# Three real products per complex product in the half-precision transforms of a state-space and SwiGLU kernel

## The chip, the cores and the metric

The kernel runs on one core of a Trainium2 chip. The metric is the device time of one execution in microseconds (us). The kernel before was run three times: 1212.44, 1216.55 and 1213.18 us, median 1213.18. A profiled execution of it has a span of 1210.1 us from its first to its last instruction.

The engines are named as the profile names them: PE is the matrix engine (PEld its weight loads), DVE the vector engine, ACT the scalar engine, POOL the GpSimd engine, SP the engine that issues most DMAs. Each engine works through its own queue in order.

## The reference

The input x has 2048 rows of 512 channels. Two layers with the same weights follow each other; each is a state-space convolution and a SwiGLU network, both with a layer norm before and a residual after:

```python
K = jnp.einsum("dn,dnl,dn->dl", Cc, P, dB).real          # P = exp(dt * A * l), complex, 128 states
Yf = rfft2(pad(u)) * rfft2(pad(K))                        # convolution over 2048 rows
y = irfft2(Yf)[..., :L] + u * Dskip
x = x + ssm(layernorm(x));   x = x + (silu(n @ w_gate) * (n @ w_up)) @ w_down   # n = layernorm(x), twice
```

The hidden width of the SwiGLU part is 1376. Everything is float32.

## The kernel before

The rows are cut into four blocks b of 512 (`T`), the channels into two halves h of 256 (`HD`). The convolution is done block by block with transforms of length 1024: the frequencies fall into four classes q of 128, and a class is one 128x128 complex matrix. For each layer, block, half and class the following is done, called a step here.

- `forward` (L229) mixes the four 128-row pieces of the normalized block on DVE into `bt` and then into the two real halves `z` (128x2x256) of a complex tile. `z` is split into a float16 part made by ACT (L250) and a float16 remainder made by DVE (L251). Twelve matmuls (four real products, each with three terms of the high and low parts, L260) give the spectrum `pf`, which ACT copies out as `u` (L262). `u` is also stored to `udr` by a DMA on POOL's queue (L637), for later blocks.
- `ssm` (L640) takes the spectra of this block and of the earlier ones and multiplies them by the kernel's spectra: `yk` and `t` hold all four real products of a complex one (128x1024, L683), L686 adds them over the blocks, and L687 and L688 make the complex result `y`, which lies in `yc`, a tile of its own. `y` is split into float16 parts `yl` by ACT (L691) and DVE (L692); twelve matmuls (L702) give the inverse transform `pi`. `combine` (L652) takes `pi` from the matrix engine's memory with one copy by ACT or two operations by DVE. After four classes, 14 operations on tiles of 256 columns (L717 to L731) add the result to x.
- `ffn` (L790) is the SwiGLU part in two pieces of 256 rows: every product is three float16 matmuls (`pgu`, L807 to L809, and `py`, L821 to L823). `pgu` goes through ACT (`sg`, L812), DVE (L813), ACT (`hh`, L814) and DVE (`hl`, L815). DVE adds `py` to x (L826).

The eight pairs of layer and block run in the order of `SEQ` (L42). For each of them the state-space part of the next pair is written ahead of the SwiGLU part of this one, so that both overlap. The first part of the program (the kernel's spectra, until about 355 us) has an order written out by hand; the rest is put in order by the framework's scheduler, which fills each engine's queue once, when the program is built. `tc.high_priority(offset=BOOST)` moves the matmuls of the transforms and the SwiGLU part's elementwise operations ahead. The forward half-precision transform is used from the third pair on (six pairs, 48 steps), the inverse one from the second (seven pairs, 56 steps). The first two pairs' spectra come from the hand-ordered part.

`BUFS` (L83) says how many buffers a name has: `y1` (the tile `yk`) and `z` have one, `t1` three; the small tiles of the matrix engine's memory (`psml`, L92) have four.

Line numbers in the profile are those of the kernel that was profiled; the changed kernel's are about ten higher.

Of the kernel before, what the change touches and what calls it, by code (L numbers as in the profile page):

```python
# [22 lines left out]
P = 128  # L23
# [4 lines left out]
HD = D // 2  # L28
# [8 lines left out]
NA = 21  # L37
TB = 256
BOOST = 1 << 20
HALF = 2  # L40
INV = 1
SEQ = ((0, 0), (0, 1), (0, 2), (1, 0), (0, 3), (1, 1), (1, 2), (1, 3))  # L42

# [1 line left out]
def dft_constants():  # L45


    j = np.arange(P)[:, None]
    r = np.arange(P)[None, :]
    ef = np.zeros((P, 4, 3, P), np.float64)  # L50
    ei = np.zeros((P, 4, 3, P), np.float64)
    ek = np.zeros((P, 4, 3, 2, P), np.float64)
    for q in range(4):
        f = q + 8 * r + 0.5
        e = np.exp(-2j * np.pi * ((j * f) / 1024.0))
        ef[:, q, 0], ef[:, q, 1], ef[:, q, 2] = e.real, e.imag, -e.real
# [12 lines left out]
    return [a.astype(np.float32) for a in (ef, ei, ek, am)] + halves  # L69
# [3 lines left out]
def kernel(ctx, tc, x, a_re, a_im, b_re, b_im, c_re, c_im, log_dt, d_skip,  # L73
# [148 lines left out]
            nc.sync.dma_start(xt, xdr[b].rearrange("c p d -> p c d"))  # L222

    def norm_x(n):
        rs, nb = row_stats(n, 4, 1.0, "stats", lambda r: tl([P, D], "junk", "t1", BF16))
        for c in range(4):
            A.activation(n[:, c], n[:, c], AF.Identity, scale=rs[:, c:c + 1], bias=nb[:, c:c + 1])

    def forward(n, h, eh):  # L229


        hs = slice(h * HD, (h + 1) * HD)
        x0, x1, x2, x3 = (n[:, c, hs] for c in range(4))
# [4 lines left out]
        A.activation(hx, x2, AF.Copy, scale=HH)  # L238
        stt(p_, x3, TT, x1, OP.add)
        stt(r_, x3, -TT, x1, OP.add)  # L240
        stt(q_, x1, TT, x3, OP.subtract)
        stt(s_, x1, TT, x3, OP.add)
        for i, q in enumerate(QORD):
            z = z2[:, 0 if eh else i % 2]
# [3 lines left out]
            if eh:  # L248
                hl = z2[:, 1].bitcast(F16).rearrange("p i (l d) -> p l i d", l=2)
                A.activation(hl[:, 0], z, AF.Copy, scale=256.0)  # L250
                stt(hl[:, 1], z, 256.0, hl[:, 0], OP.subtract)  # L251
            pf = psml([P, 2, HD], "pf")
            with tc.high_priority(offset=BOOST):
                for o in range(2):
                    if eh:
                        terms = [(eh[:, q, o + i, le], hl[:, lz, i]) for i in range(2) for le, lz in ((0, 0), (0, 1), (1, 0))]
                    else:
                        terms = [(ef[:, q, o + i], z[:, i]) for i in range(2)]
                    for k, (e, m) in enumerate(terms):
                        PE.matmul(pf[:, o], lhsT=e, rhs=m, start=k == 0, stop=k == len(terms) - 1)  # L260
                u = tl([P, 2, HD], "u", "u")
                A.activation(u, pf, AF.Copy, scale=2.0 ** -16 if eh else 1.0)  # L262
            yield q, u

    def norm_early(xt, n, factors):
        rs, nb = factors
# [344 lines left out]
    def inputs():  # L611

        for layer, b in SEQ:
# [14 lines left out]
            n = tl([P, 4, D], "n", "n")  # L628
            load_x(n, layer, b)
            norm_x(n)  # L630
            if (layer, b) == SEQ[HALF]:
                eh.append(tl([P, 4, 3, 2, P], "eh", "ef", F16))
                nc.sync.dma_start(eh[0], c_eh)
            for h in range(2):
                for q, u in forward(n, h, eh[0] if eh else None):
# [4 lines left out]
    def ssm(layer, b):  # L640
# [7 lines left out]
        for h in range(2):  # L648
# [3 lines left out]
            def combine(q, pi, bb=bb):  # L652
                if q < 2:
                    bb[q] = tl([P, 2, HD], "bb", "bb")
                    A.activation(bb[q], pi, AF.Copy, scale=sy[:, 1:2] if half else 1.0)
                    return
                s = bb[3 - q]
                bb[q] = tl([P, 2, HD], "dd", "dd")
                if half:
                    stt(bb[q], pi, sy[:, 2:3], s, OP.add)  # L660
                    stt(s, pi, sy[:, 1:2], s, OP.add)
                else:
                    V.tensor_tensor(bb[q], s, pi, OP.subtract)
                    V.tensor_tensor(s, s, pi, OP.add)

            late = []
            for _ in range(4):
# [5 lines left out]
                y = tl([P, 2, HD], "yf", "w") if first else yc  # L673
                for k in range(b + 1):
                    if k == 0:
                        w, uu = w0r[:, h, q], u
# [7 lines left out]
                                    w.unsqueeze(2).to_broadcast([P, 2, 2, HD]), OP.mult)  # L684
                    if k:
                        V.tensor_tensor(yk, yk, t, OP.add)  # L686
                V.tensor_tensor(y[:, 0], yk[:, 0, 0], yk[:, 1, 1], OP.subtract)  # L687
                V.tensor_tensor(y[:, 1], yk[:, 0, 1], yk[:, 1, 0], OP.add)  # L688
                if half:
                    yl = yl2[:, QORD.index(q) % 2]  # L690
                    A.activation(yl[:, 0], y, AF.Copy, scale=sy[:, 0:1])  # L691
                    stt(yl[:, 1], y, sy[:, 0:1], yl[:, 0], OP.subtract)  # L692
                pi = psml([P, 2, HD], "pi")
                with tc.high_priority(offset=0 if first else BOOST):
                    for o in range(2):
                        if half:
                            terms = [(eih[:, q, 0 if i == o else 1 + o, le], yl[:, ly, i])
                                     for i in range(2) for le, ly in ((0, 0), (0, 1), (1, 0))]
                        else:
                            terms = [(ei[:, q, 0 if i == o else 1 + o], y[:, i]) for i in range(2)]  # L700
                        for k, (e, m) in enumerate(terms):
                            PE.matmul(pi[:, o], lhsT=e, rhs=m, start=k == 0, stop=k == len(terms) - 1)  # L702
# [143 lines left out]
    with tc.manual_schedule(engines={mybir.EngineType.Activation, mybir.EngineType.DVE, mybir.EngineType.PE}):  # L846
# [205 lines left out]
    yl2 = tl([P, 2, 2, 2, HD], "yl2", "hf", F16)  # L1052
    xs[2] = tl([P, 4, D], "xf", "xf")
    for i, lb in enumerate(SEQ):
        if i + 1 < len(SEQ):
# [40 lines left out]
```

## Time and profile before

| what | before |
|---|---|
| median of three runs | 1213.18 us (1212.44 to 1216.55) |
| span of the profiled execution | 1210.1 us |
| PE busy | 1104.0 us (91%), 10220 matmuls |
| DVE busy | 1048.5 us (87%), 1677 instructions |
| ACT busy | 646.3 us (53%), 1392 instructions |
| POOL busy | 187.8 us (16%), 209 instructions |

The profile does not list a time of the profiled execution beside its span; the span is 3.1 us below the median of the three runs. "Busy" counts the time in which at least one instruction of an engine was under way. A row that groups instructions reads: line, engine, operation, output<-inputs, shape, count | busy us in total, mean ns of one | idle time of the engine just before them, and what ended it. A matmul's own duration (274 ns for 256 columns) is longer than the distance between two of them, since they are pipelined; a run of them in the chain of waits gives the distance. Times of POOL instructions are rough.

### The profile page before, as it was taken

Reading aid. Unit: us, or ns where it says so; the run is one execution under the profiler, and the core shown is the slowest. Engines: PE = TensorE matmul, PEld = TensorE weight load, DVE = VectorE, ACT = ScalarE, POOL = GpSimd, SP = SyncE. Lnnn points to the kernel's source line nnn. Section 1 sums busy time; section 2 is a strip of 40 time slices with the busy share of each in tenths; the row PEclk is TensorE's granted clock in tenths of the full one; section 3 lists DMA queues with packets and bytes.
Section 4 is the critical chain, followed back from the end, with each engine's and each line's share of the span. In section 5 each row is a group of like instructions: output and inputs, shape, how many; then the busy total and the mean of one; then the engine's idle time right before and its main releaser. Section 6 shows DMA issues by size and latency. Waiting matters only on the chain.

```text
span 1210.1 us, 25368 instructions
## 1 busy us (share of the span) xinstructions
PE 1104.0 (91%) x10220; PEld 858.5 (71%) x10220; DVE 1048.5 (87%) x1677; ACT 646.3 (53%) x1392; POOL 187.8 (16%) x209
## 2 busy tenths in 40 slices
PE   3877988888978998989999999999999999999998
PEld 2755766666976776868686777778686776867875
DVE  8999999999869999999998999999992799983221
ACT  7999999973265545526753524664431553324111
POOL 1116343453220010101100000121000010000000
PEclk9999998889999999999999999999999999999999
DMA  6223233236389427433245353424433144311000
GB/s 226 96 88 92 72 89 86 73 107 184 116 285 264 127 67 199 133 118 88 62 157 140 105 179 133 125 79 146 140 118 129 33 119 132 117 58 44 14 23 18
DMA packets 134857, 138.66 MB, mean 115 GB/s; under 512 B 75921, under 2 KB 85137, under 8 KB 134738
## 3 DMA queue, kind: packets, MB, share of 16 engines
q1 hardware_dynamic: 132178, 128.64, 35.4%
q0 software_dynamic: 2560, 8.39, 2.0%
q8 instruction: 80, 1.31, 0.5%
q14 instruction: 39, 0.32, 0.1%
HBM read 98.71 MB, written 28.31 MB: 105 GB/s over the span
## 4 chain that ended last, share of the span: by engine, by line
DVE 32%; PE 27%; issue 5%; DMA 4%; ACT 2%; POOL 2%; SPq 1%; DVEq 0%; ACTq 0%; POOLq 0%
DVE t L683 5%; PE pgu L807 5%; PE pgu L808 5%; PE pgu L809 5%; DVE yk L686 4%; DVE z L216 3%; DVE yk L683 3%; PE py L821 3%; PE py L822 3%; PE py L823 3%; PE pi L702 2%; DVE sg L813 2%; DVE hl L815 1%; DVE yl L216 1%; DVE bt L216 1%
## 5 line engine op out<-in xcount | busy, mean ns | idle before, releaser
L807 PE MATMUL pgu<-mix,wsl 128*128 128x256 f16 x1280 | 350.5, 274 | 7.9 <-DVE sg L813 4.4
L809 PE MATMUL pgu<-mix,wsl 128*128 128x256 f16 x1280 | 350.5, 274 | 1.2 <-DVE wsl L579 1.2
L808 PE MATMUL pgu<-mix,wsl 128*128 128x256 f16 x1280 | 350.4, 274 | 0.0
L808 PEld LDWEIGHTS <-wsl 128*128 128x128 f16 x1280 | 125.8, 98 | 24.6 <-issue 8.6
L821 PE MATMUL py<-wsl,hh 128*128 128x512 f16 (+1 forms) x352 | 134.6, 382 | 9.3 <-DVE xg L826 5.3
L809 PEld LDWEIGHTS <-wsl 128*128 128x128 f16 x1280 | 125.8, 98 | 16.5 <-DVE wsl L579 1.5
L807 PEld LDWEIGHTS <-wsl 128*128 128x128 f16 x1280 | 125.8, 98 | 15.8
L823 PE MATMUL py<-wsl,hl 128*128 128x512 f16 (+1 forms) x352 | 134.4, 382 | 2.4 <-DVE hl L815 2.4
L812 ACT ACTIVATE sg<-pgu,sc 128x512 f32<-128x512 f32 x80 | 54.5, 682 | 128.8 <-PE pgu L809 110.9
L822 PE MATMUL py<-wsl,hh 128*128 128x512 f16 x320 | 122.1, 382 | 0.0
L683 DVE TENSOR_TENSOR t<-uu,w 128x1024 f32<-128x1024 f32 x96 | 116.8, 1217 | 5.5 <-DMA uu<-udr 5.3
L686 DVE TENSOR_TENSOR yk<-yk,t 128x1024 f32<-128x1024 f32 x96 | 116.7, 1215 | 0.1
L493 PE MATMUL pw<-kt,ek 128*128 128x256 f32 (+2 forms) x420 | 105.4, 392 | 0.0
L813 DVE SCALAR_TENSOR_TENSOR sg<-pgu,sc,sg 128x512 f32<-128x512 f32 x80 | 59.6, 744 | 52.3 <-ACT sg L812 52.0
L702 PE MATMUL pi<-yl,mix 128*128 128x256 f16 x672 | 91.4, 273 | 5.5 <-ACT yl L691 3.5
L493 PEld LDWEIGHTS pw<-kt,ek 128*128 128x128 f32 x420 | 83.9, 208 | 11.9
L814 ACT ACTIVATE hh<-sg 128x512 f16<-128x512 f32 x80 | 50.0, 626 | 67.6 <-DVE sg L813 67.6
L211 POOL TENSOR_TENSOR rs<-mv,mhalf 128x2 f32<-128x2 f32 (+1 forms) x21 | 38.7, 1845 | 275.7 <-ACT mv L210 275.6
L260 PE MATMUL pf<-z,eh 128*128 128x256 f16 x576 | 74.4, 272 | 1.6 <-ACT z L250 1.6
L702 PEld LDWEIGHTS <-mix 128*128 128x128 f16 x672 | 65.3, 98 | 14.3 <-issue 3.9
L691 ACT ACTIVATE yl<-mix,sy 128x512 f16<-128x512 f32 x56 | 40.2, 717 | 61.4 <-DVE mix L688 61.2
L504 POOL COPY w0r<-s 128x128 f32<-128x128 f32 x29 | 48.1, 1659 | 141.7 <-ACT s L502 122.2
(221 smaller groups left out, 2292.0 us busy)
## 6 DMA issues: line engine op xcount, KB each, us to landing
w<-wdr SPq DMA_DIRECT2D x96, 256.0 KB, 2.8
uu<-udr SPq DMA_DIRECT2D x96, 256.0 KB, 3.0
udr<-u POOLq DMA_DIRECT2D x32, 256.0 KB, 2.8
wdr<-wo SPq DMA_DIRECT2D x96, 64.0 KB, 2.0
udr<-u SPq DMA_DIRECT2D x16, 256.0 KB, 2.5
n<-ndr SPq DMA_DIRECT2D x16, 256.0 KB, 3.0
n<-xdr SPq DMA_DIRECT2D x4, 1024.0 KB, 6.0
xg<-in_A_u_dram SPq DMA_DIRECT2D x3, 1024.0 KB, 7.4
```

Of the source, the lines that this page charges most:

```text
L260: PE.matmul(pf[:, o], lhsT=e, rhs=m, start=k == 0, stop=k == len(terms) - 1)
L493: PE.matmul(pw[:, i], lhsT=e, rhs=kt[:, :, c + 4 * k0:4 * k1:4, :].rearrange("p g k d -> p k g d"), start=c == 0, stop=c == 3)
L683: V.tensor_tensor(t, uu.unsqueeze(1).to_broadcast([P, 2, 2, HD]), w.unsqueeze(2).to_broadcast([P, 2, 2, HD]), OP.mult)
L686: V.tensor_tensor(yk, yk, t, OP.add)
L702: PE.matmul(pi[:, o], lhsT=e, rhs=m, start=k == 0, stop=k == len(terms) - 1)
L807: PE.matmul(o, lhsT=wgu(wi, k, 0)[:, fs], rhs=nh[:, k], start=k == 0, stop=False)
L808: PE.matmul(o, lhsT=wgu(wi, k, 0)[:, fs], rhs=nlo[:, k], start=False, stop=False)
L809: PE.matmul(o, lhsT=wgu(wi, k, 1)[:, fs], rhs=nh[:, k], start=False, stop=k == 3)
L813: V.scalar_tensor_tensor(sg, pgu[:, 1], sc6[:, 4:5], sg, OP.mult, OP.mult)
L821: PE.matmul(py[:, r], lhsT=hh[:n, f, rc], rhs=wd(f, 0)[:n], start=f == 0, stop=False)
L822: PE.matmul(py[:, r], lhsT=hh[:n, f, rc], rhs=wd(f, 1)[:n], start=False, stop=False)
L823: PE.matmul(py[:, r], lhsT=hl[:n, f, rc], rhs=wd(f, 0)[:n], start=False, stop=f == FT - 1)
```

## The change

Each complex product of the two half-precision transforms is done with three real products in place of four. For a complex number with the parts z0 and z1 and a matrix with the parts fr and fi, the forward transform becomes

    first part  = (fr - fi) z0 + fi (z0 + z1)
    second part = (-fr - fi) z1 + fi (z0 + z1)

and the inverse one has the same form. The tables `eh` and `eih` hold these three matrices. A new function `three` issues nine matmuls (three real products of three terms): two products go into `pb`, the shared one into `pa`; ACT copies both out, and POOL adds `a` to both halves. The sum z0+z1 and its float16 split are made by POOL in the forward transform (`zsum`, in the place of `yc`); in the inverse one POOL makes the sum, and ACT and DVE split three tiles of 256 columns at once. `y` now lies in `yk` itself. The factor 256, which was applied when `z` was split, is now in the layer norm of `norm_x`. `yl` has one buffer of three parts in place of two buffers of two.

```diff
-    for e in (ef * 256.0, ei * 8192.0):
+    fr, fi, ir, ii = ef[:, :, 0], ef[:, :, 1], ei[:, :, 0], ei[:, :, 1]
+    for e in (np.stack([fi, fr - fi, -fr - fi], 2) * 256.0, np.stack([ir, ii - ir, -ir - ii], 2) * 8192.0):
...
-        rs, nb = row_stats(n, 4, 1.0, "stats", lambda r: tl([P, D], "junk", "t1", BF16))
+        rs, nb = row_stats(n, 4, 256.0, "stats", lambda r: tl([P, D], "junk", "t1", BF16))
...
+        zs, hs2 = zsum[:, 0], zsum[:, 1].bitcast(F16).rearrange("p (l d) -> p l d", l=2)
...
-                A.activation(hl[:, 0], z, AF.Copy, scale=256.0)
-                stt(hl[:, 1], z, 256.0, hl[:, 0], OP.subtract)
-            pf = psml([P, 2, HD], "pf")
+            A.activation(hl[:, 0], z, AF.Copy)
+            V.tensor_tensor(hl[:, 1], z, hl[:, 0], OP.subtract)
+            G.tensor_tensor(zs, z[:, 0], z[:, 1], OP.add)
+            G.tensor_copy(hs2[:, 0], zs)
+            G.tensor_tensor(hs2[:, 1], zs, hs2[:, 0], OP.subtract)
             with tc.high_priority(offset=BOOST):
-                ... (12 matmuls into pf)
                 u = tl([P, 2, HD], "u", "u")
-                A.activation(u, pf, AF.Copy, scale=2.0 ** -16 if eh else 1.0)
+                three(eh[:, q], (hl[:, :, 0], hl[:, :, 1], hs2), u, 2.0 ** -16)
             yield q, u
+
+    def three(e, parts, o, scale):
+        pb = psml([P, 2, HD], "pb")
+        pa = psml([P, 2, HD], "pa")
+        for d, w, m in ((pb[:, 0], 1, parts[0]), (pb[:, 1], 2, parts[1]), (pa[:, 0], 0, parts[2])):
+            for k, (le, lz) in enumerate(((0, 0), (0, 1), (1, 0))):
+                PE.matmul(d, lhsT=e[:, w, le], rhs=m[:, lz], start=k == 0, stop=k == 2)
+        a = tl([P, HD], "a", "t1")
+        A.activation(o, pb, AF.Copy, scale=scale)
+        A.activation(a, pa[:, 0], AF.Copy, scale=scale)
+        G.tensor_tensor(o, o, a.unsqueeze(1).to_broadcast([P, 2, HD]), OP.add)
...
+                if half:
+                    y = yk.rearrange("p a b d -> p (a b) d")[:, :3]
+                    V.tensor_tensor(y[:, 0], yk[:, 0, 0], yk[:, 1, 1], OP.subtract)
+                    V.tensor_tensor(y[:, 1], yk[:, 0, 1], yk[:, 1, 0], OP.add)
+                    G.tensor_tensor(y[:, 2], y[:, 0], y[:, 1], OP.add)
+                    yl = tl([P, 2, 3, HD], "yl", "hf", F16)
+                    A.activation(yl[:, 0], y, AF.Copy, scale=sy[:, 0:1])
+                    stt(yl[:, 1], y, sy[:, 0:1], yl[:, 0], OP.subtract)
+                    bb[q] = tl([P, 2, HD], "bb", "bb") if q < 2 else tl([P, 2, HD], "dd", "dd")
+                    with tc.high_priority(offset=BOOST):
+                        three(eih[:, q], [yl[:, :, i] for i in (1, 0, 2)], bb[q], sy[:, 1:2])
+                    if q > 1:
+                        s = bb[3 - q]
+                        V.tensor_tensor(s, s, bb[q], OP.add)
+                        stt(bb[q], bb[q], -2.0, s, OP.add)
+                    yield
+                    continue
...
-        yc = mix[:, 3 * D:4 * D].rearrange("p (i d) -> p i d", i=2)
+        zsum = mix[:, 3 * D:4 * D].rearrange("p (i d) -> p i d", i=2)
```

The instructions stand in these orders, at three places.

DVE, the 28th inverse step (pair (0, 3), third earlier block), from the end of `y` on; `yl` is the float16 remainder, `yk<-u,w0r` the first product of the next step, `sg` and `hl` the SwiGLU part's. Before:

```order
L687 TENSOR_TENSOR mix<-yk 128x256
L688 TENSOR_TENSOR mix<-yk 128x256
L683 TENSOR_TENSOR t<-uu,w 128x1024
L683 TENSOR_TENSOR yk<-u,w0r 128x1024
L216 SCALAR_TENSOR_TENSOR yl_3763<-mix,sy,yl_3763 128x512
L813 SCALAR_TENSOR_TENSOR sg<-pgu,sc_92,sg 128x512
L686 TENSOR_TENSOR yk<-yk,t 128x1024
L815 TENSOR_TENSOR hl<-sg,hh 128x512
```

and in the change:

```order
L691 TENSOR_TENSOR yk<-yk 128x256
L692 TENSOR_TENSOR yk<-yk 128x256
L685 TENSOR_TENSOR t<-uu,w 128x1024
L824 SCALAR_TENSOR_TENSOR sg<-pgu,sc_92,sg 128x512
L216 SCALAR_TENSOR_TENSOR yl<-yk,sy,yl 128x768
L826 TENSOR_TENSOR hl<-sg,hh 128x512
L685 TENSOR_TENSOR yk<-u,w0r 128x1024
L688 TENSOR_TENSOR yk<-yk,t 128x1024
```

The next step's first product stood ahead of the remainder `yl`; now it stands behind it, and `yl` is half as wide again.

POOL, where the spectra of the second layer's first pair (`udr_115`) are stored: before, a stretch with the stores of `u`, the exponent of a layer norm (`rs<-mv,mhalf`) and the clearing of `sgr`:

```order
L211 TENSOR_TENSOR rs<-mv,mhalf 128x2
L637 DMA udr_114<-u 128x512 x4
L211 TENSOR_TENSOR rs<-mv,mhalf 128x4
L781 MEMSET sgr 128x4x32
L637 DMA udr_114<-u 128x512
L637 DMA udr_115<-u 128x512 x4
```

and in the change (`mix<-z` is the sum z0+z1, `mix<-mix` its two float16 parts, `yk<-yk` the sum of `y`, `u<-u,a` and `bb<-bb,a` the additions of the shared product):

```order
L693 TENSOR_TENSOR yk<-yk 128x256
L254 TENSOR_TENSOR mix<-mix 128x256
L270 TENSOR_TENSOR u<-u,a 128x512
L252 TENSOR_TENSOR mix<-z_3762 128x256
L644 DMA udr_115<-u 128x512
L253 CAST mix<-mix 128x256
L254 TENSOR_TENSOR mix<-mix 128x256
L693 TENSOR_TENSOR yk<-yk 128x256
L252 TENSOR_TENSOR mix<-z_3762 128x256
L211 TENSOR_TENSOR rs<-mv,mhalf 128x2
L270 TENSOR_TENSOR bb<-bb,a 128x512
L270 TENSOR_TENSOR u<-u,a 128x512
```

Each forward step has brought four operations to POOL's queue and each inverse step two; the layer norm's exponent and the stores stand between them.

PE, from the last matmul of the last inverse transform on: before,

```order
L702 MATMUL pi<-yl_3763,mix 128x256
L809 LDWEIGHTS wsl_3322
L809 MATMUL pgu<-mix,wsl_3322 128x256
L807 LDWEIGHTS wsl_3322
L807 MATMUL pgu<-mix,wsl_3322 128x256
```

and in the change:

```order
L266 MATMUL pa<-yl,mix 128x256
L832 LDWEIGHTS hh
L832 MATMUL py<-wsl_3324,hh 128x512
L833 LDWEIGHTS hh
L833 MATMUL py<-wsl_3324,hh 128x512
```

Behind the last inverse matmul stood 988 matmuls, in the middle of the second last pair's SwiGLU part; now there are 741, and they begin with the last output products of that part.

More of the change, by code (lines that the diff above doesn't have):

```diff
@@ L39 @@
 BOOST = 1 << 20
-HALF = 2
 INV = 1
@@ L242, in forward @@
         stt(s_, x1, TT, x3, OP.add)
+        zs, hs2 = zsum[:, 0], zsum[:, 1].bitcast(F16).rearrange("p (l d) -> p l d", l=2)
         for i, q in enumerate(QORD):
-            z = z2[:, 0 if eh else i % 2]
+            z = z2[:, 0]
             u_, v_ = ((p_, a_) if q in (0, 3) else (q_, b_))
@@ L630, in inputs @@
             norm_x(n)
-            if (layer, b) == SEQ[HALF]:
+            if not eh:
                 eh.append(tl([P, 4, 3, 2, P], "eh", "ef", F16))
@@ L634, in inputs @@
             for h in range(2):
-                for q, u in forward(n, h, eh[0] if eh else None):
+                for q, u in forward(n, h, eh[0]):
                     if b < NB - 1:
@@ L654, in combine @@
                     bb[q] = tl([P, 2, HD], "bb", "bb")
-                    A.activation(bb[q], pi, AF.Copy, scale=sy[:, 1:2] if half else 1.0)
+                    A.activation(bb[q], pi, AF.Copy)
                     return
@@ L658, in combine @@
                 bb[q] = tl([P, 2, HD], "dd", "dd")
[L659 to L664, printed above, removed]
+                V.tensor_tensor(bb[q], s, pi, OP.subtract)
+                V.tensor_tensor(s, s, pi, OP.add)
             late = []
@@ L672, in ssm @@
                 yk = tl([P, 2, 2, HD], "yk", "y1")
-                y = tl([P, 2, HD], "yf", "w") if first else yc
                 for k in range(b + 1):
@@ L687, in ssm @@
+                y = tl([P, 2, HD], "yf", "w")
                 V.tensor_tensor(y[:, 0], yk[:, 0, 0], yk[:, 1, 1], OP.subtract)
                 V.tensor_tensor(y[:, 1], yk[:, 0, 1], yk[:, 1, 0], OP.add)
[L689 to L692, printed above, removed]
                 pi = psml([P, 2, HD], "pi")
[L694 to L702, printed above, removed]
+                for o in range(2):
+                    terms = [(ei[:, q, 0 if i == o else 1 + o], y[:, i]) for i in range(2)]
+                    for k, (e, m) in enumerate(terms):
+                        PE.matmul(pi[:, o], lhsT=e, rhs=m, start=k == 0, stop=k == len(terms) - 1)
```

11 lines of the change are left out of this document (1 added, 10 removed).

## The prediction

> **What bounds the kernel now.** I read first the page's busy times, then a table by stage, cut where the stretches with another bound begin.
>
> ```profile
> PE 1104.0 (91%) x10220; PEld 858.5 (71%) x10220; DVE 1048.5 (87%) x1677; ACT 646.3 (53%) x1392; POOL 187.8 (16%) x209
> ```
>
> ```profile
> core 0: us, PE busy (x) PEld busy (x) DVE busy (x) ACT busy (x) POOL busy (x), PEclk, DMA share, GB/s
> 0.00:395.00 395.00, 317.88 (x3666) 254.31 (x3667) 373.15 (x561) 297.90 (x718) 129.16 (x143) 0.94 0.45 137
> 395.00:907.00 512.00, 491.72 (x4144) 384.10 (x4142) 499.77 (x844) 253.45 (x495) 50.95 (x56) 0.99 0.41 125
> 907.00:952.00 45.00, 44.41 (x373) 33.53 (x370) 15.46 (x29) 17.27 (x37) 1.34 (x1) 1.00 0.29 95
> 952.00:1082.00 130.00, 126.88 (x1055) 95.08 (x1053) 123.11 (x184) 44.80 (x83) 4.59 (x5) 1.00 0.35 104
> 1082.00:1210.10 128.10, 123.12 (x992) 91.43 (x989) 36.98 (x62) 32.90 (x60) 1.80 (x4) 0.99 0.09 25
> ```
>
> The average of 91% and 87% hides who leads. From 395 to 907 us DVE is busy 499.8 of 512 us, PE nearly as much. From 907 to 952 DVE stands for 29.5 us, and the timeline of DVE says for what:
>
> ```profile
> 925.46 0.75 DVE L826 SCALAR_TENSOR_TENSOR xg<-py,sc,xg 128x512 f32<-128x512 f32 x1 [5.41 <-PE py L823]
> 940.94 0.75 DVE L813 SCALAR_TENSOR_TENSOR sg<-pgu,sc,sg 128x512 f32<-128x512 f32 x1 [7.31 <-ACT sg L812]
> ```
>
> It waits for PE to finish a SwiGLU part that is late. Then DVE is full again until the last inverse transform at 1082 us, and 128 us of SwiGLU work on PE remain. So DVE sets the pace of the transforms, and PE has a backlog, paid once at 907 (29.5 us) and once at the end. POOL is nearly empty after 395 us.
>
> **PE: what goes.** The distance between the transforms' matmuls stands in the chain of waits:
>
> ```profile
> 539.16 1.31 PE pf L260 x12
> 1081.17 1.20 PE pi L702 x11
> ```
>
> That is 109 ns each. Of the groups by line
>
> ```profile
> L702 PE MATMUL pi<-yl,mix 128*128 128x256 f16 x672 | 91.4, 273 | 5.5 <-ACT yl L691 3.5 <-DVE yl L216 2.0
> L260 PE MATMUL pf<-z,eh 128*128 128x256 f16 x576 | 74.4, 272 | 1.6 <-ACT z L250 1.6
> ```
>
> a quarter goes: 168 + 144 = 312 matmuls, 34 us of PE. Where DVE leads, they are worth nothing.
>
> **DVE: its own work.** The rows:
>
> ```profile
> L686 DVE TENSOR_TENSOR yk<-yk,t 128x1024 f32<-128x1024 f32 x96 | 116.7, 1215 | 0.1
> L216 DVE SCALAR_TENSOR_TENSOR yl<-mix,sy,yl 128x512 f16<-128x512 f32 x56 | 41.6, 743 | 2.2 <-ACT yl L691 2.1
> L216 DVE SCALAR_TENSOR_TENSOR z<-z 128x512 f16<-128x512 f32 x48 | 32.8, 683 | 2.1 <-ACT z L250 2.1
> L815 DVE TENSOR_TENSOR hl<-sg,hh 128x512 f16<-128x512 f32 x80 | 54.8, 684 | 14.0 <-ACT hh L814 13.9
> L216 DVE SCALAR_TENSOR_TENSOR dd<-pi,sy,bb 128x512 f32<-128x512 f32 x28 | 20.8, 743 | 3.5 <-PE pi L702 3.4
> ```
>
> 512 further columns cost 1215 - 684 = 531 ns, so `yl` with 256 more costs 0.27 us more, 56 times: +15 us. The two operations that combined `pi` (743 ns each) become two in the style of the rows of 684 and 683 ns: 28 x 0.12 = -3 us. The remainder of `z` changes from a row of 683 to one of 684 ns: nothing. Own work: **+12 us**.
>
> **POOL, and what it does to DVE.** The change brings 48 x 4 + 56 x 2 = 304 operations to POOL. What one costs alone is seen at 335 us, where DVE has nothing to do:
>
> ```profile
> 335.14 0.32 POOL L513 TENSOR_TENSOR wo<-s,w0r 128x64 f32<-128x64 f32 x1
> 335.42 0.46 POOL L514 TENSOR_TENSOR wo<-s 128x128 f32<-128x128 f32 x1
> ```
>
> 2.2 ns an element and 0.18 us beside: 0.74 us for 256 columns with two inputs, 1.3 us for 512. The one-input cast lies between 0.3 us (the shortest copy of 128 columns, 0.29 below) and 0.74; I take 0.43. A forward step is 3.2 us, an inverse step 2.0 us, 268 us in all, and POOL has some 700 us for it. Would that be all, it would be free. It isn't, by the groups and the timeline of the stretch in which POOL and DVE worked side by side:
>
> ```profile
> L445 DVE TENSOR_TENSOR g<-g,tmp 128x64 f32<-128x64 f32 x8 | 3.4, 425 | 0.0
> L445 DVE TENSOR_TENSOR g<-g,tmp 128x128 f32<-128x128 f32 x8 | 2.3, 284 | 0.0
> L510 POOL TENSOR_TENSOR wo<-s 128x192 f32<-128x192 f32 x58 | 61.8, 1085 | 0.0
> L504 POOL COPY w0r<-s 128x128 f32<-128x128 f32 x29 | 48.1, 1659 | 141.7 <-ACT s L502 122.2 <-DMA st<-in_B_w_up_dram 16.4 <-DMA wdr<-wo 3.0
> ```
>
> ```profile
> 160.74 0.27 DVE L430 TENSOR_TENSOR g<-g,tmp 128x64 f32<-128x64 f32 x1
> 164.05 0.68 DVE L445 TENSOR_TENSOR g<-g,tmp 128x64 f32<-128x64 f32 x1
> 164.65 0.69 DVE L446 TENSOR_TENSOR g<-g,tmp 128x64 f32<-128x64 f32 x1
> ```
>
> ```profile
> 162.76 0.29 POOL L504 COPY w0r<-s 128x128 f32<-128x128 f32 x1 [2.90 <-ACT s L502]
> 163.01 2.19 POOL L510 TENSOR_TENSOR wo<-s 128x192 f32<-128x192 f32 x2
> ```
>
> A DVE operation on half the elements takes longer, on average, than the full one. In the timeline each of the two POOL operations adds 0.41 us to the DVE operation beside it (0.68 for 0.27), and takes 1.1 us itself where 0.18 + 192 x 2.2 ns = 0.60 would do. So here an addition on POOL and a DVE operation with two inputs from the same memory exclude each other, for 0.41 / 192 = 2.1 ns an element, and who comes second waits. The copies of 128 columns took 1659 ns on average, and DVE operations beside copies are not longer, so I give the cast 0.2 us, between nothing and 0.55.
>
> DVE's time that this may take: a forward step 0.55 (sum) + 0.2 + 0.55 (remainder) + 1.09 (the addition of 512 columns) = 2.4 us, 48 times 115 us; an inverse step 0.55 + 1.09 = 1.64 us, 56 times 92 us. Together 207 us: the upper end. Nothing is the lower end, if all falls into DVE's pauses or beside operations with one input from there:
>
> ```profile
> L813 DVE SCALAR_TENSOR_TENSOR sg<-pgu,sc,sg 128x512 f32<-128x512 f32 x80 | 59.6, 744 | 52.3 <-ACT sg L812 52.0
> L826 DVE SCALAR_TENSOR_TENSOR xg<-py,sc,xg 128x512 f32<-128x512 f32 x24 | 17.9, 746 | 37.8 <-PE py L823 37.8
> ```
>
> These are about 75 us in the stretch, of which I let half hide POOL work, 37 us; the pauses from 395 to 907 and from 952 to 1082 are 12 + 7 us, half of them 10; half of the new pause below, 35. Seen on DVE: 207 - 82 = **+125 us**.
>
> **The new wait.** `y` now lies in `yk`, so the next step's first product can't start before `yl` is done, and `yl` waits for POOL's sum and a split by ACT of 768 columns. In the order DVE starts a `t` product of 1.14 us right behind `y`, which shuts POOL out for that long. Then 0.74 us on POOL, and ACT:
>
> ```profile
> L691 ACT ACTIVATE yl<-mix,sy 128x512 f16<-128x512 f32 x56 | 40.2, 717 | 61.4 <-DVE mix L688 61.2
> L379 ACT ACTIVATE re<-im 128x1024 f32<-128x1024 f32 x16 | 17.6, 1102 | 6.4 <-DVE im L372 6.3
> L262 ACT ACTIVATE u<-pf 128x512 f32<-128x512 f32 x48 | 28.3, 589 | 58.8 <-PE pf L260 58.7
> L238 ACT ACTIVATE bt<-n 128x256 f32<-128x256 f32 x12 | 4.9, 407 | 9.0 <-DVE z L216 9.0
> ```
>
> 0.91 us for 768 columns, between the first two rows; with hand-overs of about 0.05 us that makes 2.86 us. What stands between `y` and `yl` on DVE covers some of it: in the step shown in the order `t` and `sg`, 1.14 + 0.67 = 1.81, which leaves 1.05 us. Counted so over all 56 steps of the order, 42 us remain. That is the lower end, with POOL free at that moment; an addition of 512 columns ahead of the sum in POOL's queue costs 1.3 us more, 56 times 73 us. I take 0.4 of such a case: **+65 us** (42 to 115). Behind the waiting `yl` DVE holds `sg` and `hl` of the SwiGLU part, so PE's next matmuls wait too; in POOL's queue the layer norm's exponent and the stores of `u` stand behind additions that wait for ACT. The stores are read one pair later, tens of us away.
>
> ACT gets 48 + 56 copies of `a`, 28 more copies of 512 columns and the wider `yl`: 104 x 0.41 + 28 x 0.59 + 56 x 0.19, about 70 us by these rows; it is busy 253 of 512 us, so it hides them while DVE leads.
>
> **The sum.** DVE's stretch grows by 12 + 125 + 65 = 202 us. It takes up PE's backlog: the pause of 29.5 us at 907, and at the end the 247 matmuls that now stand ahead of the last inverse transform (988 behind it before, 741 now), at 109 ns for 256 columns and twice that for 512, about 30 us. 1210 + 202 - 60 = 1352 us of span. The median of the runs lies 3 us above the profiled span: **1355 us**, 12% slower.
>
> Here a rule of the Trainium skill ("SBUF — State Buffer", section "SBUF: two separate sides") goes further than the row of 0.41 us: a GpSimd operation that reads SBUF and a DVE operation with two SBUF inputs take a shared pair of ports as an exclusive lock, for the whole instruction. Taken at its word, each such POOL operation costs DVE all its time and not 2.1 ns an element.
>
> **The rivals.**
>
> *The exclusion lasts the whole POOL instruction* (what that rule says). Then DVE loses up to the 268 us above in place of 207; with the same share seen (125 of 207), 162 us, and the time is 1392. Against it stands the 0.41 us, where 0.60 would be the whole. Chance 0.08.
>
> *POOL hides.* Its work falls into DVE's new pauses and beside `sg`, and only own work and the new wait remain: 1210 + 12 + 65 - 60 = 1227, with the 3 us 1230. For it speaks that a pause of a microsecond a step is just where POOL's queue is full; against it that POOL's 268 us don't fit into 65 + 75 + 19 us. Chance 0.14 (1217 to 1290).
>
> *PE leads after all* (the other side: faster). The 34 us of PE count, DVE's growth stays below the 60 us of backlog: 1210 - 34 + 3 = 1179. For it: PE is busy 96% from 395 to 907 and it is PE that DVE waits for at 907. It decides as soon as DVE grows by less than 60 us, that is if exclusion and new wait together stay below 48 of the 272 us that I count for them. Chance 0.12.
>
> *POOL's queue leads.* Each of 304 operations may be kept waiting as the copies were (1659 for about 300 ns), and each is a link in a chain that DVE waits for. With all 207 us seen and a pause of 3.3 us a step (185 us): 1210 + 12 + 207 + 185 - 60 + 3 = 1557. Chance 0.09 (above 1440).
>
> **How the numbers follow.** The forecast has 0.54 and lies from 1290 to 1440 us, by half to nearly all of the exclusion seen; with the rival of 1392, which lies in the same stretch, 0.62. A measurement of this kernel tells about 0.3% (4 us) from no change. Faster is PE's rival, 0.12; 0.03 I leave for a tie of the gains and losses; slower 0.85. The range of 8 in 10 goes from 1210 to 1440: it leaves out PE's rival and most of POOL's. Left to the likeliest case alone it would be 1290 to 1440.
>
> **What would show it.** DVE's operations with 1024 columns longer than 1215 ns on average, by about 0.4 us beside each addition of POOL; POOL's additions of 256 columns above 0.74 us, those of 512 above 1.3; a row in which `yl` waits for ACT some 50 us or more, where it waited 2.1; no pause of DVE for PE at 907; a tail of about 97 us behind the last inverse matmul; PE busy 34 us less in work but with waits for `yl` and `mix`. I am wrong if the mean of 1024 columns stays at 1215 ns (no exclusion between these operations), or if DVE's pauses in the stretch stay below 5%.

## The result: 17% slower, and the profile after

| | before | changed |
|---|---|---|
| median | 1212.81 us (1207.95 to 1216.55, 4 runs) | 1418.64 us (1417.99 to 1420.55, 4 runs) |
| span of the profiled execution | 1210.1 us | 1416.8 us |

The ratio is 1.170, with a 95% interval from 1.166 to 1.174. The busy times of the changed kernel, from the page of its profile:

```profile
PE 1125.7 (79%) x9908; PEld 847.6 (60%) x9908; DVE 1211.4 (86%) x1677; ACT 708.5 (50%) x1524; POOL 605.7 (43%) x513
```

DVE issues as many instructions as before, 1677, and is busy 163 us longer. PE has the 312 matmuls less that were meant to go.

The table by stage, with columns as in the prediction, cut at the last `y` of the last inverse step. First the kernel before:

```profile
395.00:1076.60 681.60, 657.60 (x5524) 508.56 (x5522) 636.51 (x1053) 314.79 (x613) 56.88 (x62) 0.99 0.39 119
1076.60:1210.10 133.50, 128.52 (x1034) 95.59 (x1032) 38.81 (x66) 33.62 (x61) 1.80 (x4) 0.99 0.09 26
```

And the same two rows of the changed kernel:

```profile
395.00:1303.60 908.60, 711.28 (x5485) 524.46 (x5483) 809.30 (x1069) 381.06 (x752) 448.39 (x360) 0.90 0.30 90
1303.60:1416.80 113.20, 99.03 (x757) 70.93 (x755) 31.37 (x55) 29.01 (x53) 3.90 (x5) 0.94 0.09 27
```

The stretch in which DVE leads has grown by 227.0 us: DVE is busy 172.8 us longer in it (809.3 for 636.5) and stands 54.2 us longer (99.3 for 45.1). The tail is 20.3 us shorter. Together 206.7 us, the whole difference of the spans.

Where DVE's time went shows in its groups by line and shape, and POOL's beside them:

```profile
L685 DVE TENSOR_TENSOR t<-uu,w 128x1024 f32<-128x1024 f32 x96 | 128.7, 1340 | 6.2 <-DMA uu<-udr 5.8
L688 DVE TENSOR_TENSOR yk<-yk,t 128x1024 f32<-128x1024 f32 x96 | 131.3, 1368 | 0.8
L216 DVE SCALAR_TENSOR_TENSOR z<-bt 128x256 f32<-128x256 f32 x96 | 64.7, 706 | 1.5 <-POOL mix L253 0.5
L824 DVE SCALAR_TENSOR_TENSOR sg<-pgu,sc,sg 128x512 f32<-128x512 f32 x80 | 59.3, 742 | 32.2 <-ACT sg L823 32.2
L216 DVE SCALAR_TENSOR_TENSOR yl<-yk,sy,yl 128x768 f16<-128x768 f32 x56 | 58.8, 1049 | 46.3 <-ACT yl L695 45.9
L693 POOL TENSOR_TENSOR yk<-yk 128x256 f32<-128x256 f32 x56 | 92.2, 1646 | 177.1 <-DVE yk L692 168.5
L270 POOL TENSOR_TENSOR u<-u,a 128x512 f32<-128x512 f32 x48 | 86.4, 1800 | 12.8 <-ACT a L269 12.6
```

Two of these groups in the kernel before, which the prediction doesn't show:

```profile
L683 DVE TENSOR_TENSOR t<-uu,w 128x1024 f32<-128x1024 f32 x96 | 116.8, 1217 | 5.5 <-DMA uu<-udr 5.3
L216 DVE SCALAR_TENSOR_TENSOR z<-bt 128x256 f32<-128x256 f32 x96 | 36.3, 416 | 0.1
```

The operations of 1024 columns take 1340 and 1368 ns (before 1217 and 1215), and `z`, whose own code hasn't changed, 706 ns for 416. `sg`, whose one input lies in the matrix engine's memory, takes 742 ns for 744: it isn't touched. POOL's sum of 256 columns takes 1646 ns where 740 had been worked out.

The timelines show one meeting of the two engines, DVE first, then POOL:

```profile
503.24 2.89 DVE L216 SCALAR_TENSOR_TENSOR z<-bt 128x256 f32<-128x256 f32 x2
```

```profile
503.08 1.36 POOL L270 TENSOR_TENSOR dd<-dd,a 128x512 f32<-128x512 f32 x1 [1.44 <-ACT a L269]
504.41 1.44 POOL L270 TENSOR_TENSOR u<-u,a 128x512 f32<-128x512 f32 x1
```

Two operations of 416 ns that overlap a little (0.75 us for both) take 2.89 us beside two additions of 512 columns: 2.14 us more, 1.07 us for each addition, 2.1 ns an element. (The first addition had begun 0.16 us before the DVE operation.)

### The profile page after: what moved, and what is told of

Same layout as the page of the kernel before. It is cut to its first block, busy times and chain, and to the rows that moved or that the text cites. A ratio compares the mean times of both kernels' runs of the same rounds, so it can differ in the third digit from the quotient of the medians.

```text
span 1416.8 us, 25335 instructions
## 1 busy us (share of the span) xinstructions
PE 1125.7 (79%) x9908; PEld 847.6 (60%) x9908; DVE 1211.4 (86%) x1677; ACT 708.5 (50%) x1524; POOL 605.7 (43%) x513
## 4 chain that ended last, share of the span: by engine, by line
DVE 40%; PE 11%; issue 8%; POOL 8%; ACT 6%; DMA 3%; SPq 1%; DVEq 0%; POOLq 0%; ACTq 0%
DVE yk L688 6%; DVE t L685 5%; DVE yk L685 4%; POOL yk L693 4%; DVE z L216 3%; DVE z L251 2%; DVE yl L216 2%; ACT yl L695 2%; DVE hl L826 2%; DVE sg L824 2%; PE py L834 2%; PE py L832 2%; DMA mix<-nn 2%; PE py L833 2%; PE pgu L819 1%
## 5 line engine op out<-in xcount | busy, mean ns | idle before, releaser
L818 PE MATMUL pgu<-mix,wsl 128*128 128x256 f16 x1280 | 354.4, 277 | 24.5 <-DVE sg L824 16.3
L820 PE MATMUL pgu<-mix,wsl 128*128 128x256 f16 x1280 | 353.9, 277 | 1.7 <-DVE wsl L586 1.7
L819 PE MATMUL pgu<-mix,wsl 128*128 128x256 f16 x1280 | 354.1, 277 | 0.0
L693 POOL TENSOR_TENSOR yk<-yk 128x256 f32<-128x256 f32 x56 | 92.2, 1646 | 177.1 <-DVE yk L692 168.5
L266 PE MATMUL pb<-yl,mix 128*128 128x256 f16 x336 | 60.6, 295 | 102.2 <-ACT yl L695 90.8
L685 DVE TENSOR_TENSOR t<-uu,w 128x1024 f32<-128x1024 f32 x96 | 128.7, 1340 | 6.2 <-DMA uu<-udr 5.8
L688 DVE TENSOR_TENSOR yk<-yk,t 128x1024 f32<-128x1024 f32 x96 | 131.3, 1368 | 0.8
L695 ACT ACTIVATE yl<-yk,sy 128x768 f16<-128x768 f32 x56 | 52.3, 934 | 157.1 <-POOL yk L693 157.0
L266 PEld LDWEIGHTS <-mix 128*128 128x128 f16 x504 | 52.6, 105 | 119.9 <-issue 108.2
L252 POOL TENSOR_TENSOR mix<-z 128x256 f32<-128x256 f32 x48 | 72.5, 1511 | 88.2 <-DVE z L216 88.1
L216 DVE SCALAR_TENSOR_TENSOR yl<-yk,sy,yl 128x768 f16<-128x768 f32 x56 | 58.8, 1049 | 46.3 <-ACT yl L695 45.9
L270 POOL TENSOR_TENSOR u<-u,a 128x512 f32<-128x512 f32 x48 | 86.4, 1800 | 12.8 <-ACT a L269 12.6
```

The costliest lines, as they stand in the source:

```text
L216: V.scalar_tensor_tensor(o, i0, s, i1, OP.mult, op1)
L266: PE.matmul(d, lhsT=e[:, w, le], rhs=m[:, lz], start=k == 0, stop=k == 2)
L685: V.tensor_tensor(t, uu.unsqueeze(1).to_broadcast([P, 2, 2, HD]), w.unsqueeze(2).to_broadcast([P, 2, 2, HD]), OP.mult)
L693: G.tensor_tensor(y[:, 2], y[:, 0], y[:, 1], OP.add)
L818: PE.matmul(o, lhsT=wgu(wi, k, 0)[:, fs], rhs=nh[:, k], start=k == 0, stop=False)
L819: PE.matmul(o, lhsT=wgu(wi, k, 0)[:, fs], rhs=nlo[:, k], start=False, stop=False)
```

## The experiments

The theory: an operation of POOL that reads two pieces of memory and one of DVE that does so exclude each other, so the work given to POOL is paid by DVE. The rival: POOL runs beside DVE, and the new waits (`yl` for POOL's sum, the tile `yk` that is held) make the time. Times are medians; every ratio is to the kernel before on the same chip, where its median lay between 1212.7 and 1215.5 us.

### Useless work on POOL, in the kernel before

Additions that nobody waits for:

```diff
                 A.activation(u, pf, AF.Copy, scale=2.0 ** -16 if eh else 1.0)
+            for _ in range(10):
+                G.tensor_tensor(ident, u[:, 0, :P], u[:, 1, :P], OP.add)
             yield q, u
```

> The kernel before, with ten useless additions of 128 columns on POOL in each of the 48 forward steps; each reads two pieces of u and writes a tile that nobody reads, so no engine waits for their results. Exclusion: 480 x 128 x 2.1 ns = 131 us of DVE's time, 80 to 130 us seen, less 30 to 45 us of backlog: 1260 to 1300 us, and DVE's operations of 1024 columns longer than 1215 ns. Waiting: 1213 us, 1215 ns.

1303.40 us, ratio 1.073 (1.068 to 1.078), 3 us above the range that was expected. Groups by line of this run, and its table by stage:

```profile
L264 POOL TENSOR_TENSOR ident<-u 128x128 f32<-128x128 f32 x480 | 411.0, 856 | 203.9 <-ACT u L262 171.5
L685 DVE TENSOR_TENSOR t<-uu,w 128x1024 f32<-128x1024 f32 x96 | 125.8, 1311 | 5.6 <-DMA uu<-udr 5.4
L688 DVE TENSOR_TENSOR yk<-yk,t 128x1024 f32<-128x1024 f32 x96 | 124.3, 1294 | 0.1
```

```profile
395.00:1168.20 773.20, 681.11 (x5528) 513.88 (x5527) 730.71 (x1052) 315.16 (x613) 450.78 (x542) 0.97 0.35 105
1168.20:1301.10 132.90, 127.93 (x1031) 95.31 (x1029) 38.84 (x66) 33.64 (x61) 1.81 (x4) 1.00 0.09 26
```

DVE has no new wait (it stands 159.0 us in all, before 161.6), no complex product has changed, and the kernel is 91 us longer in span: DVE is busy 94 us more (1142.1 us in all, on the page of its profile). That is the exclusion by itself. The time lies above the expected range because no backlog was taken up: the tail is still 132.9 us (133.5 before), and DVE's pauses for PE are still there, only later:

```profile
1003.17 0.75 DVE L828 SCALAR_TENSOR_TENSOR xg<-py,sc,xg 128x512 f32<-128x512 f32 x1 [5.41 <-PE py L825]
1018.68 0.75 DVE L815 SCALAR_TENSOR_TENSOR sg<-pgu,sc,sg 128x512 f32<-128x512 f32 x1 [7.35 <-ACT sg L814]
```

Two pauses of this length (5.41 and 7.31 us) stood at 925 and 941 us before. So a later DVE didn't take up PE's backlog. In both programs 988 matmuls stand behind the last inverse transform: PE's queue is written once, SwiGLU matmuls behind transforms, and PE falls behind together with DVE. In the stretch it stands 92.1 us (773.2 - 681.1), before 24.0 (681.6 - 657.6).

Copies in place of the additions:

```diff
+            for _ in range(10):
+                G.tensor_copy(ident, u[:, 0, :P])
```

> The kernel before with ten useless copies of 128 columns on POOL in each forward step, one input each. If every read of POOL shuts out DVE for its elements, at half the price of an addition: 480 x 0.14 = 65 us, less 40 us of backlog, 1225 to 1250 us. If copies give way to DVE, as the copies of the first part that took 1659 ns did, 1213 us, and the copies are long.

1241.84 us, ratio 1.024 (1.017 to 1.030). DVE is busy 1075.1 us, 27 us more; its two rows of 1024 columns read 1237 and 1234 ns. The time lies in the expected range, but by luck: 65 us less 40 us of backlog had been counted, and it was 27 us with no backlog taken up. Copies do exclude DVE, for 27 us / 480 = 55 ns each (0.43 ns an element), where the additions took 94 / 480 = 195 ns (1.5 ns an element, part of them beside pauses and `sg`).

Fills in their place, which read nothing:

```diff
+            G.tensor_copy(ident[:, :2], u[:, 0, :2])
+            for _ in range(10):
+                G.memset(ident, 0.0)
```

> The kernel before with ten useless fills of 128 columns on POOL in each forward step, which read nothing (one copy of two columns ahead of them keeps their place). If only reads of POOL shut out DVE: 1213 us and 1215 ns for 1024 columns. If any POOL work does: 480 x 0.2 = 96 us less 40, 1270 us.

1227.58 us, ratio 1.012 (1.005 to 1.019): slower by more than expected, but not by exclusion:

```profile
L686 DVE TENSOR_TENSOR t<-uu,w 128x1024 f32<-128x1024 f32 x96 | 116.8, 1217 | 4.8 <-DMA uu<-udr 4.6
L689 DVE TENSOR_TENSOR yk<-yk,t 128x1024 f32<-128x1024 f32 x96 | 116.7, 1216 | 0.1
L265 POOL MEMSET ident<- 128x128 f32 x480 | 98.9, 206 | 25.7
```

DVE's rows are those of before, its busy time 1049.2 us (before 1048.5), and the fills take 206 ns. Some 15 us come from elsewhere, and DVE stands for them (178.8 us in all for 161.6); DVE's wait for the layer norm's exponent in POOL's queue is 15.5 us in this run and 9.4 before, and the rest stays open.

### The change's POOL work done by DVE

```diff
-            G.tensor_tensor(zs, z[:, 0], z[:, 1], OP.add)
-            G.tensor_copy(hs2[:, 0], zs)
-            G.tensor_tensor(hs2[:, 1], zs, hs2[:, 0], OP.subtract)
+            V.tensor_tensor(zs, z[:, 0], z[:, 1], OP.add)
+            A.activation(hs2[:, 0], zs, AF.Copy)
+            V.tensor_tensor(hs2[:, 1], zs, hs2[:, 0], OP.subtract)
...
-        G.tensor_tensor(o, o, a.unsqueeze(1).to_broadcast([P, 2, HD]), OP.add)
+        V.tensor_tensor(o, o, a.unsqueeze(1).to_broadcast([P, 2, HD]), OP.add)
...
-                    G.tensor_tensor(y[:, 2], y[:, 0], y[:, 1], OP.add)
+                    V.tensor_tensor(y[:, 2], y[:, 0], y[:, 1], OP.add)
```

> The change with everything that it gave to POOL done by DVE (the cast by ACT): both sums, the remainder of the sum, the addition of the shared product. By rows of 416 ns for 256 and 684 ns for 512 columns DVE gets 48 x 0.83 + 56 x 0.42 + 104 x 0.68 = 134 us more work. Exclusion: in exchange about 160 us of stretched operations and most of the waits for POOL go, so it is not slower than the change: 1340 to 1400 us. If POOL's work had run beside DVE's: 1418 + 134 less some waits, 1490 to 1550 us.

1364.13 us, ratio 1.123 (1.118 to 1.129): 54 us faster than the change, with 256 more instructions on the engine that leads. Groups by line:

```profile
L688 DVE TENSOR_TENSOR yk<-yk,t 128x1024 f32<-128x1024 f32 x96 | 116.8, 1217 | 0.7
L685 DVE TENSOR_TENSOR t<-uu,w 128x1024 f32<-128x1024 f32 x96 | 116.7, 1216 | 4.6 <-DMA uu<-udr 4.2
L216 DVE SCALAR_TENSOR_TENSOR z<-bt 128x256 f32<-128x256 f32 x96 | 36.3, 416 | 0.0
L216 DVE SCALAR_TENSOR_TENSOR yl<-yk,sy,yl 128x768 f16<-128x768 f32 x56 | 56.7, 1013 | 17.7 <-ACT yl L695 17.1
```

All rows are back at their old lengths, and the wait of `yl` falls from 46 to 17 us. DVE is busy 1181.9 us, 30 us less than when POOL did the work. Had POOL's work run beside DVE's, this run would have been the slower one.

### The change without that work

```diff
-            G.tensor_tensor(zs, z[:, 0], z[:, 1], OP.add)
-            G.tensor_copy(hs2[:, 0], zs)
-            G.tensor_tensor(hs2[:, 1], zs, hs2[:, 0], OP.subtract)
...
-                three(eh[:, q], (hl[:, :, 0], hl[:, :, 1], hs2), u, 2.0 ** -16)
+                three(eh[:, q], (hl[:, :, 0], hl[:, :, 1], hl[:, :, 0]), u, 2.0 ** -16)
...
-        G.tensor_tensor(o, o, a.unsqueeze(1).to_broadcast([P, 2, HD]), OP.add)
...
-                    G.tensor_tensor(y[:, 2], y[:, 0], y[:, 1], OP.add)
```

> The change without any of its work on POOL: the sum z0+z1 and its split, the sum of y and the addition of the shared product are left out (the third product takes a part that is there already), so the output is not the reference's; the nine matmuls, the copies by ACT and the wider yl stay. Exclusion: everything but 12 us of DVE's own work and some microseconds of waiting of yl for ACT goes; 708 matmuls stand behind the last inverse transform in place of 988, and PE has 312 matmuls less: 1170 to 1205 us. If the tile that is held, the order or ACT's copies were what the change costs: 1230 us or more.

1235.71 us, ratio 1.019 (1.014 to 1.024). The expected gain isn't there: the time lies where the expectation had put the held tile, the order or ACT's copies. That is a rival for 26 us of span, not for the whole. The busy times:

```profile
PE 1081.4 (88%) x9908; PEld 832.0 (67%) x9908; DVE 1064.3 (86%) x1677; ACT 709.6 (57%) x1524; POOL 176.1 (14%) x209
```

POOL's part of the change is then 1416.8 - 1235.9 = 181 us of span, of which 147 us are longer DVE operations (1211.4 - 1064.3). The other 26 us are what the change costs with its sums for nothing: 16 us of DVE's own work, and about 10 us of pauses (22 us more ahead of the tail, 12 us fewer in the tail, which is 113.1 us long for 133.5). `yl` waits 5.8 us in all here, so the tile that is held isn't the cause by itself; which part of the pauses is ACT's added work and which the new order wasn't separated. And the 34 us of PE bring no gain: with nine matmuls in place of twelve, the kernel is still slower.

### One transform alone

Forward by three products, the inverse one by four. `y`, the twelve matmuls into `pi` and the combination of `bb` are written as before the change; the place for the forward sums moves to the second half of `yl2`:

```diff
-    for e in (np.stack([fi, fr - fi, -fr - fi], 2) * 256.0, np.stack([ir, ii - ir, -ir - ii], 2) * 8192.0):
+    for e in (np.stack([fi, fr - fi, -fr - fi], 2) * 256.0, ei * 8192.0):
...
-                    y = yk.rearrange("p a b d -> p (a b) d")[:, :3]
...
-                    G.tensor_tensor(y[:, 2], y[:, 0], y[:, 1], OP.add)
-                    yl = tl([P, 2, 3, HD], "yl", "hf", F16)
+                    yl = yl2[:, 0]
...
+    yl2 = tl([P, 2, 2, 2, HD], "yl2", "hf", F16)
+    zsum = yl2[:, 1].rearrange("p l i d -> p (l i d)").bitcast(F32).rearrange("p (i d) -> p i d", i=2)
```

> Only the forward transform uses three products; the inverse one keeps four, with y in its own tile and one buffer of yl. Exclusion (POOL's additions take DVE's time, as the prediction has it): POOL's lock time here is 115 of the 207 us; of the 207, about 160 us showed in the changed kernel's DVE rows, so about 90 us here; less the backlog of PE (about 45 us): 1260 us (1235 to 1290), operations of 1024 columns longer than 1215 ns. Waiting (the rival: the cost is the wait of yl for POOL's sum, and POOL runs freely beside DVE): there is no such wait here, so 1195 to 1215 us and 1215 ns.

1264.41 us, ratio 1.041 (1.036 to 1.046): as expected, though two counts were off against each other. DVE is busy 67 us more (1115.9) where 90 were expected, and stands 15 us less (146.8 for 161.6) where 45 us of backlog were. Of its operations of 1024 columns the sums `yk` are longer (1270 ns), the products `t` aren't (1215).

The inverse one by three, the forward one by four, with its split of `z` and its twelve matmuls into `pf` as before the change:

```diff
-    for e in (np.stack([fi, fr - fi, -fr - fi], 2) * 256.0, np.stack([ir, ii - ir, -ir - ii], 2) * 8192.0):
+    for e in (ef * 256.0, np.stack([ir, ii - ir, -ir - ii], 2) * 8192.0):
...
+                    for k, (e, m) in enumerate(terms):
+                        PE.matmul(pf[:, o], lhsT=e, rhs=m, start=k == 0, stop=k == len(terms) - 1)
```

> Only the inverse transform uses three products, as in the change. Exclusion: 92 of the 207 us of lock time, 72 of them seen, 12 us of own work and 45 us of waits of yl, less 45 us of backlog: 1297 us (1265 to 1330). Waiting: 12 + 45 us less the backlog: 1213 to 1230 us if POOL runs freely; if the wait is the whole cost of the change, 1380 to 1420 us.

1340.40 us, ratio 1.104 (1.095 to 1.113): 10 us above the range that was expected, and between the two that the rival had. DVE is busy 69 us more (1117.6) and stands 63 us more (224.7 for 161.6; in the stretch 106 for 45); `yl` waits 42.5 us for ACT, and a wait of 18.7 us for `u` hadn't been counted. With the inverse transform alone the waits add nearly as much as the longer work.

The same with `y` and its sum in tiles of their own:

```diff
-                    y = yk.rearrange("p a b d -> p (a b) d")[:, :3]
+                    y, yl, y2 = zsum, hf[:, :1536].rearrange("p (l i d) -> p l i d", l=2, i=3), hf[:, 1536:].bitcast(F32)
...
-                    G.tensor_tensor(y[:, 2], y[:, 0], y[:, 1], OP.add)
+                    G.tensor_tensor(y2, y[:, 0], y[:, 1], OP.add)
...
+                    A.activation(yl[:, 0, :2], y, AF.Copy, scale=sy[:, 0:1])
+                    A.activation(yl[:, 0, 2], y2, AF.Copy, scale=sy[:, 0:1])
+                    stt(yl[:, 1, :2], y, sy[:, 0:1], yl[:, 0, :2], OP.subtract)
+                    stt(yl[:, 1, 2], y2, sy[:, 0:1], yl[:, 0, 2], OP.subtract)
```

> As the run with the inverse transform alone, but y and the sum lie in tiles of their own, so the next step's first product needn't wait for yl; ACT and DVE split y in two pieces (56 x about 0.2 us more each). Exclusion: the same lock time, without most of the 45 us of waits: 20 to 40 us below that run, 1260 to 1280 us. If the wait for the tile is the main cost: below 1230 us.

1313.66 us, ratio 1.083 (1.076 to 1.089): 27 us below the run with the held tile, inside the 20 to 40 us that were expected between the two. DVE has 10 us more work in it (1127.7 for 1117.6), so the held tile is worth some 27 to 37 us here, and the run is still 100 us of span above the kernel before (1310.6 for 1210.1). The absolute time missed, since it was counted from 1297 us for the run before, which took 1340.

### The shared product added by PE

```diff
-        pa = psml([P, 2, HD], "pa")
-        for d, w, m in ((pb[:, 0], 1, parts[0]), (pb[:, 1], 2, parts[1]), (pa[:, 0], 0, parts[2])):
-            for k, (le, lz) in enumerate(((0, 0), (0, 1), (1, 0))):
-                PE.matmul(d, lhsT=e[:, w, le], rhs=m[:, lz], start=k == 0, stop=k == 2)
-        a = tl([P, HD], "a", "t1")
+        for i in range(2):
+            k = 0
+            for w, m in ((1 + i, parts[i]), (0, parts[2])):
+                for le, lz in ((0, 0), (0, 1), (1, 0)):
+                    PE.matmul(pb[:, i], lhsT=e[:, w, le], rhs=m[:, lz], start=k == 0, stop=k == 5)
+                    k += 1
         A.activation(o, pb, AF.Copy, scale=scale)
-        A.activation(a, pa[:, 0], AF.Copy, scale=scale)
-        G.tensor_tensor(o, o, a.unsqueeze(1).to_broadcast([P, 2, HD]), OP.add)
```

> The change, but PE adds the shared product to both halves (twelve matmuls again), so POOL keeps only the sums and their float16 split, and ACT has one copy. Exclusion: POOL's lock time falls from 207 to 93 us, of which 72 are seen; with 12 us of own work and 45 us of waits of yl, less 45 us of backlog: 1297 us (1270 to 1330). Waiting (the chain y, POOL's sum, ACT, yl is the cost): that chain is untouched, so 1390 to 1420 us. If the missing PE work were what matters: 34 us more than the change, 1450 us.

1312.02 us, ratio 1.081 (1.070 to 1.093): 107 us faster than the change, though PE does 312 matmuls more. The time lies in the range that was expected. The wait of `yl` is, at 51.4 us, no shorter than in the change, so the chain through POOL's sum isn't what the 107 us were.

## Why the prediction was right, and which term was off

The forecast of 1355 us was on the right side and its range held the 1418.64 us; the change was 206 us and not 142. The mechanism, DVE held up by POOL's reads, is the one that the runs show. Two terms are off by some 26 us each, the backlog and the waits that were put at nothing; two more, the exclusion and the wait of `yl`, are off by about 20 us in opposite directions and cancel by luck. Term by term, in us of span:

| term | predicted | measured, and where |
|---|---|---|
| DVE's own work | +12 | +16 (DVE's busy time without POOL's work, 1064.3 for 1048.5) |
| exclusion by POOL, seen on DVE | +125 of 207 | +147 (1211.4 - 1064.3) |
| new wait of `yl` | +65 (42 to 115) | +44 (45.9 for 2.1 in DVE's waits for `yl`) |
| PE's backlog taken up | -60 | -34: 14 in the stretch (`sg` for ACT and `xg` for PE, 22.7 to 8.2), 20 in the tail |
| other new waits of DVE | 0 | +26 in the stretch: `z` for ACT 8, `bt` for ACT 8, `yk` for POOL's `u` 6, `nn` and `rs` 4 |

These add up to 199 of the 206.7 us; DVE does 7.4 us less work in the tail than before (31.4 for 38.8), so that much of the 20 only moved ahead of the cut.

**The exclusion** was the right mechanism, at the right price: 2.1 ns an element in the 0.41 us rows of the first part and 1.07 us for 512 columns in the change's timeline. What was off was the share that hides: I let 82 of 207 us hide; if the 207 hold, it was 60. The four runs on POOL's kind of work (additions +88 us, copies +29, fills +15 without any longer DVE operation, and the work moved to DVE -54) show it by itself. The variant in which DVE loses the whole POOL instruction would have had 1.3 us for an addition of 512 columns; the meeting in the timeline shows 1.07. With the 0.16 us by which the first addition was ahead that is 1.15 at most, and one meeting doesn't decide between the two. The copies lie further from the whole instruction: one cost DVE 55 ns on average, where the shortest took 290 ns itself, and an addition cost 195 ns of about 460. The Trainium skill's rule ("SBUF — State Buffer", section "SBUF: two separate sides") agrees in which operations exclude each other, here also that fills don't; in the length of the lock the rows stay nearer to 2.1 ns an element than to the whole instruction.

**The backlog** was sized at 60 us and gave 34. "It takes up PE's backlog" took the 29.5 us of pauses and 30 us of the tail as time that a slower DVE gets for nothing. The run with useless additions shows that this isn't so where the order stays nearly the same: 94 us more of DVE, 91 us more of span, the same tail, the same pauses. PE's waits (us in total, times, longest) say why. Before, then in the run with additions:

```profile
PE pi L702 <- ACT yl L691: 3.5, 5, 1.5
PE pi L702 <- DVE yl L216: 2.0, 4, 1.2
PE py L823 <- DVE hl L815: 2.4, 2, 1.3
```

```profile
PE pi L704 <- ACT yl L693: 16.7, 19, 4.1
PE pi L704 <- DVE yl L216: 13.6, 16, 3.9
PE py L825 <- DVE hl L817: 10.2, 7, 3.1
```

PE waits longer for what DVE makes (`yl` also for ACT's part of it), in the transforms and in the SwiGLU part, so the time that a slower DVE leaves it isn't used to work off the backlog. In the change itself the order was made anew, with 741 matmuls behind the last inverse transform, and part of the backlog did go. DVE's three long pauses for PE (5.4, 5.3 and 7.3 us around 930 us) are gone; in the whole stretch it waits at most 2.4 us for `py`. PE has no work left at times:

```profile
PE pb L266 <- ACT yl L695: 90.8, 28, 18.9
```

```profile
480.52 0.37 PE L266 MATMUL pb<-yl,mix 128*128 128x256 f16 x1 [18.94 <-ACT yl L695]
488.10 0.26 PE L785 MATMUL pgu<-wsl,mix 128*128 128x96 f16 x1 [3.74 <-DMA mix<-nn]
```

At the longest of these waits the SwiGLU part before it has ended, and the first matmuls of the next one (`pgu`, L785) then still wait 3.7 us for their own rows. The tail got shorter by 20 us; behind the last inverse matmul it is 109 us long where the prediction had 97 (before 128). PE waits there for the last layer norm's transposes (`PE pgu L785 <- DMA mix<-nn`, 6.1 us once, and 1.9 us more for L787), and its granted clock is lower (0.70 from 1308 to 1330 us).

**The new wait** was over-priced: 45.9 us of DVE's waits, near the lower end of 42. Of the extra of 23 us for additions ahead of the sum in POOL's queue little is seen. Other waits stand there that the sum put at nothing: `z` for ACT (10.3 us for 2.1), `bt` for ACT (9.0 for 1.4), `yk` for POOL's `u` (6.2, before 0.3 for ACT's `u`). What delays ACT in them wasn't separated.

**ACT** was put at nothing. It is busy 708.5 us for 646.3, and DVE's waits for its copies of `u` and `a` aren't among the ten longest of the change. That it hides altogether isn't shown: in the run without POOL's work, from 395 us to the tail, DVE waits 26 us more than before for ACT in five places (`bt` 10.7 us for 1.4, `sgr` 5.6 for 1.5, `bb` 5.1 for 0, `yl` 4.8 for 1.3, `yk` 4.3 for 0.3), by ACT's added work or by the new order.

**The signs.** The longer operations of 1024 columns, POOL's longer additions and the end of the pauses for PE came as foretold. `yl` waits a little less than the 50 us. PE's busy time didn't fall by 34 us but rose by 22 (1125.7 for 1104.0): its matmuls are recorded longer, 295 ns for `pb` where `pi` had 273, while its granted clock in the stretch was 0.90 for 0.99.

The rivals: POOL hiding is refuted by 147 us of longer operations. PE leading is refuted by the run without POOL's work, where PE's 312 matmuls are gone and the kernel is still 26 us longer in span. POOL's queue leading isn't seen: in the stretch POOL is busy 448 of 909 us, and its longest waits are for DVE's `y` (152.0 us) and `z` (88.1).

## What to carry to other kernels

An engine that looks idle isn't free if its reads and those of the engine that leads hold each other up: look for operations of one shape that are longer beside the idle engine's work (here 425 ns for 64 columns, 284 ns for 128) and charge that price. Work given up on PE, which didn't lead, was worth nothing here. And the backlog of an engine with a fixed queue isn't a sure reserve: with nearly the same order none of it was taken up when the leading engine got slower, and with a new order a little over half of what was counted.

## What the runs showed of the hardware that wasn't expected

- DVE is held up by POOL's copies too, at 0.43 ns an element (27 us for 480 copies of 128 columns), though the prediction had read no longer DVE operations beside the copies of the first part. The 29 copies there, at 55 ns each, would cost 1.6 us, an estimate too small to be seen in those rows. Fills leave DVE alone (1217 and 1216 ns for 1024 columns).
- POOL's operations get longer as well beside a busy DVE: a copy of two columns took 1733 ns on average in the run with fills, where the shortest copy of 128 columns in the kernel before took 290, and a sum of 256 columns 1646 ns in the change, where 740 were worked out from rows without DVE.
- PE's granted clock was 0.90 in the change's long stretch (0.99 before), where PE has more pauses, and 0.50 from 1320 to 1330 us behind 10 us in which it was busy 5.04. Whether the lower clock adds to the time wasn't separated.
